# adaLN block on one Trainium2 core: how the first layer norm of the third and fourth chunks is turned from rows into columns

## The chip, the cores and the metric

The kernel runs on one core of a Trainium2 chip. The metric is the device time of one execution in microseconds (us): the median of several runs. The profile is one execution, recorded by the hardware profiler. Engines are named as the profile names them: PE is TensorE's matmul side and PEld its weight load, DVE is VectorE, ACT is ScalarE, POOL is GpSimd, SP is SyncE, which issues every DMA here.

## The reference

```python
x = A_x                                          # 1 x 2048 x 512, fp32
sa, ca, ga, sb, cb, gb = silu(c) @ w_mod         # six vectors of 512
h = layernorm(x) * (1 + ca) + sa
q, k, v = h @ wqkv                               # 32 heads of 16
phi = lambda t: where(t > 0, t + 1, exp(t)) + 1e-6
kv = einsum("bhsd,bhse->bhde", phi(k), v);  z = sum over s of phi(k)
o = (phi(q) @ kv) / (phi(q) . z + 1e-6)
x = x + ga * (o @ wo)
h = layernorm(x) * (1 + cb) + sb
x = x + gb * (((h @ w_gate) * (h @ w_up)) @ w_down)
```

## The kernel before

The 2048 tokens are four chunks of 512 (`NCH`), each of four tiles of 128 tokens (`NJ`); a tile is 128 partitions by 512 features. Tile number i runs from 0 to 15 and is `ch, j = divmod(i, 4)`. Every matrix product is done in three matmuls of high and low parts: an operand f is split into h, its rounded copy (fp32r), and l = f - h, and the product is hh + hl + lh (`product`, L207 to L209). So each operand costs one copy and one subtraction, which ACT, DVE or POOL do.

The order of the work on every engine is written out by hand: the program text is the order, each engine takes its own instructions strictly in that order, and semaphores join the engines. All SBUF tiles come from one pool of 94 buffers (`NB`). PSUM has four banks from `bank()` and four accumulators from `acc_bank()`.

The change lies in the loop over i (L525 to L587), the key stage. An iteration i does, in this order:

- PE: the projection of the keys of tile i + 2 (`proj(i + 2, wk)`, 12 matmuls), in iterations 3, 4, 6 and 7 also that of the queries of one of tiles 0 to 3 (12 matmuls), and `t_tile(i)` (12 matmuls, L373 to L375), which adds x-hat times phi(k) of tile i to the four accumulators.
- ACT and DVE: `k_split_x(i + 1)` and `k_split(i + 1)`, the parts of x-hat and of phi(k) that `t_tile(i + 1)` reads (L194, L195, L364, L365); `k_phi(i + 2)`, which makes phi of the projected keys (two ACT instructions, L337 and L338, and DVE L341); the same for the queries (`q_a`, `q_b`); and `z_add`, the running sum of phi(k) (DVE L358).
- `extra[i]`: work for later stages, such as the splits of `wv` (iterations 4 to 7), the sums for the modulation vectors (`mod_part`, DVE L162 and L164), the loads for them (`mod_load`, on SP's queue) and the splits of `wo`.

`proj` reads a chunk's modulated, transposed rows as pairs (h, l) in `norm[ch].t[k]`, one pair for each of four blocks of 128 features. The first projection that reads chunk 2 is `proj(8, wk)` in iteration 6, and the first that reads chunk 3 is `proj(12, wk)` in iteration 10. Each begins with block k = 0 and takes three matmuls for a block.

How a later chunk's pairs come about, before (chunk 2 in iterations 2 to 5, chunk 3 in 6 to 9):

1. In iteration j = 2 of the chunk two ahead of it, DVE takes the statistics of its tiles 0 and 1, and at j = 3 of tiles 2 and 3 (`stats`, L242 and L243). Then POOL makes the four reciprocal standard deviations at once (`rstd_of`, L262 and L263), DVE the four products with the mean (`nmr_of`, L267), and ACT x-hat of tiles 0 and 1 (`xhat`, L272).
2. At j = 0 of the chunk before it, ACT makes x-hat of tiles 2 and 3.
3. At j = 0 and at j = 1 (`turn_at`, `turn_x`), between the first six and the last six matmuls of `t_tile`, PE transposes two feature blocks of the four tiles, eight matmuls of 128 by 128 (L293), into two PSUM banks; ACT reads each bank once with scale and bias (L305), DVE makes h (L313) and l (L316).

In later stages the kernel already turns other tiles without PE: `stow` and `unstow`, or `move_out` and `move_in`, send a tile to DRAM and read it back in another order of its 32 by 32 blocks; DVE transposes each block in place (L736, L901; the tile `wide` holds a chunk), and `flipped` (L907) lets ACT read one feature block out of `wide` with scale and bias. `xhat_blocks` (L279) writes x-hat with its columns grouped for that.

After the loop the tail of the stage scales the accumulators (L655, L656), splits them (L658 to L660) and multiplies them with `wv` (L667), while PE is covered by `proj(6, wq)` and `proj(7, wq)`.

Of the kernel before, what the change touches and what calls it, by code (L numbers as in the profile page):

```python
# [14 lines left out]
P = 128  # L15
NB = 94
BL = 32
# [7 lines left out]
def tile_adaln_block(  # L25
# [291 lines left out]
                self.t[k] = (h, l)  # L317


    NT = NCH * NJ  # L320
    norm = [Norm(xts[0])]
    wk, wq, wv = [], [], []
# [20 lines left out]
    def k_split_x(i):  # L343
        ch, j = divmod(i, NJ)
        kx[i] = [B("xh", dt=F32R), B("xl", dt=F32R)]
        split(norm[ch].n[j], *kx[i])

    def k_phi(i, ps):
        phi = B("phi")
# [154 lines left out]
    def mod_part(v, *ks):  # L504
        if 0 in ks:
# [11 lines left out]
             12: lambda: (mod_part(4, 2, 3), wo_s.extend(split_raw(x) for x in raw_o[:2]), cols.update({3: col_out(3, mod_col(accs[3], bank()), 0.0)}), mod_load(5)),  # L517
             13: lambda: (mod_part(5, 0, 1, 2), wo_s.extend(split_raw(x) for x in raw_o[2:]), cols.update({4: col_out(4, mod_col(accs[4], bank()), 1.0)})),
             14: lambda: (mod_part(5, 3),)}
    pairs = {}  # L520
    q_at = {3: 0, 4: 1, 6: 2, 7: 3}
    ahead = {2: k_ps[2], 3: k_ps[3]}
    turn_at = {4 * ch + j: (ch + 1, 2 * j, 2 * j + 1) for ch in range(1, NCH - 1) for j in range(2)}
    turn_at.update({1: (1, 0, 1), 2: (1, 2, 3)})
    for i in range(NT):  # L525
        ch, j = divmod(i, NJ)
        done = 0
        if i > 2:
            ahead[i + 2] = proj(i + 2, wk) if i + 2 < NT else proj(i + 6 - NT, wq)
        if i in q_at:  # L530
# [7 lines left out]
        fresh = i > 0 and ch + 1 < NCH and j == 0  # L538
        if i == 2:
            turn_x()  # L540
            wq.extend(split_blocks(r) for r in raw_q)
        if fresh:
            nx.xhat(2)
        if 0 < i < NT - 1:
            k_split_x(i + 1)
        if fresh:
            nx.xhat(3)
        if 0 < i < NT - 1:
            k_split(i + 1)
        if i in turn_at and i != 2:  # L550
            t_tile(i, 0, 1)
            done = 2
            turn_x()
        if i == 2:
            t_tile(i, *range(KD))
            done = KD
            ahead[i + 2] = proj(i + 2, wk)
        if ch + 2 < NCH and j == 2:
            nx2 = Norm(xts[ch + 2])
            nx2.stats(0, 1)  # L560
        if ch + 2 < NCH and j == 3:
            nx = nx2
# [12 lines left out]
        if i + 1 < NT:  # L575
            z_add(i + 1)
        if i == NT - 2:
            pairs["z"] = split_raw(zacc, low=nc.gpsimd)
        if i == NT - 1:
            zps = row_sum(pairs["z"])  # L580
            zb = consts.tile([P, D], F32, name="zb")
            nc.scalar.activation(zb, zps, AF.Identity, bias=eps_z)
            zq = B("z")
            nc.gpsimd.tensor_copy(zq.rearrange("p (q s i) -> p q s i", q=NQ, i=BL), by_block(zb))
        t_tile(i, *range(done, KD))
        if i in extra:
            extra[i]()  # L587
    ga, sb, cb = rows[2], cols[3], cols[4]
# [130 lines left out]
    def move_out(*tiles):  # L719

        for i in tiles:
            moved[i] = tc.dram_tile([P, D], F32, name=f"moved_{i}")
            nc.sync.dma_start(moved[i], phq.pop(i))

    def move_in(*tiles):

        for i in tiles:
            v = moved[i].rearrange("(m i) (q c) -> q i m c", i=BL, c=P)
            moved[i] = B("u")
            for q in range(NQ):  # L730
                nc.sync.dma_start(moved[i][q * BL:(q + 1) * BL].rearrange("i (m c) -> i m c", c=P), v[q])

    def turn_v(i):

# [163 lines left out]

    def flip(ch, *js):
        for j in js:  # L900
            nc.vector.transpose(wide[:, j].rearrange("p (m s i) -> p m s i", m=NQ, i=BL),  # L901
                                blocks.pop((ch, j)).rearrange("p (m s i) -> p m s i", m=NQ, i=BL))

    def flipped(ch, *ks):
        for k in ks:
            f = B("f")
            nc.scalar.activation(f.rearrange("p (x i) -> p x i", i=BL),  # L907
                                 wide.rearrange("p j (m s i) -> p (j m) s i", m=NQ, i=BL)[:, :, k],
                                 AF.Identity, scale=cb[:, k:k + 1], bias=sb[:, k:k + 1])
            blocks[ch, "f", k] = f  # L910

    stowed, blocks = {}, {}

# [403 lines left out]
    first[0].sum("s1", "s3", on=nc.gpsimd)  # L1317
    g(lambda: turn_v(13))
    y_seed(13, y_bank)
    norm2[2].xhat_blocks(2, 3)  # L1320
    turn_h(13)
    turn_l(13)
    move_in(14, 15)
    stow(2, 0, 1, 2, 3)
# [107 lines left out]
```

## Time and profile before

| | us |
|---|---|
| median of 3 runs (554.28 to 555.3) | 554.39 |
| the profiled execution's own time | 554.37 |
| its span, first to last instruction | 552.7 |
| PE busy in the span | 547.0 |
| DVE busy | 373.6 |
| ACT busy | 291.7 |
| POOL busy | 203.4 |

The span is the stretch from the first to the last instruction that the profiler saw, and the 1.67 us beside it are the start and the end of the execution. Busy time is the union of an engine's instructions. A row of the timeline gives the start, the duration, the engine, the line of the kernel, what it writes and reads, and in brackets how long the engine had been idle before it and who ended that. Instructions of one engine overlap by about a tenth of a microsecond at their edges, so the distance from one start to the next is what counts in a queue.

### The profile page before, as it was taken

What the parts mean: (1) busy time and instruction counts of PE and PEld (TensorE: products, weight loads), DVE (VectorE), ACT (ScalarE), POOL (GpSimd) and SP (SyncE); (2) the same over time, 40 slices, a digit from 0 to 9 for tenths busy, and PEclk for the clock granted to TensorE, in tenths of its full rate; (3) what the DMA queues carried; (4) which work ended last, traced back from release to release, by engine and by line L of the source; (5) the groups of instructions that cost most, each with busy time, mean ns of one, the idle gap of its engine ahead of it and who ended that gap; (6) DMA issues with size and microseconds to landing.
All of it is one profiled execution on the core that took longest, in us unless ns stands there. A gap on an engine that the chain in (4) does not pass through costs nothing.

```text
span 552.7 us, 7324 instructions
## 1 busy us (share of the span) xinstructions
PE 547.0 (99%) x2488; PEld 449.2 (81%) x2488; DVE 373.6 (68%) x610; ACT 291.7 (53%) x539; POOL 203.4 (37%) x204
## 2 busy tenths in 40 slices
PE   8999999999999999999999999999999999999997
PEld 7788888888888878878888888877888888888886
DVE  7896968986887886778776576985444444434434
ACT  3695856646476667566684545454443444444110
POOL 2000000102003201057596666766666546446200
PEclk9999999999999999999999999999999999999999
DMA  8900203320503205845545071690434222200004
GB/s 284 387 15 2 76 20 103 108 77 1 157 2 133 96 5 186 267 145 135 160 111 155 0 230 38 216 322 2 133 116 132 59 57 59 58 20 0 1 0 152
DMA packets 58373, 58.28 MB, mean 105 GB/s; under 512 B 7328, under 2 KB 38304, under 8 KB 58336
## 3 DMA queue, kind: packets, MB, share of 16 engines
q1 hardware_dynamic: 58336, 57.83, 33.2%
q8 instruction: 19, 0.31, 0.2%
q14 instruction: 18, 0.15, 0.1%
HBM read 42.60 MB, written 15.20 MB: 105 GB/s over the span
## 4 chain that ended last, share of the span: by engine, by line
PE 99%; DVE 0%; issue 0%
PE bank L1030 33%; PE acc L766 7%; PE acc L1110 6%; PE acc L1111 6%; PE acc L1112 6%; PE bank L207 5%; PE bank L209 5%; PE bank L208 5%; PE acc L375 3%; PE acc L374 3%; PE acc L373 3%; PE bank L849 2%; PE bank L851 2%; PE bank L850 2%; PE acc L146 2%; PE bank L293 2%
## 5 line engine op out<-in xcount | busy, mean ns | idle before, releaser
L1030 PE MATMUL bank<-h,w 128*128 128x512 f32 (+1 forms) x798 | 184.7, 390 | 0.0
L1030 PEld LDWEIGHTS bank<-h,w 128*128 128x128 f32 (+1 forms) x798 | 148.4, 186 | 33.4 <-ACT bank L1035 0.7
L1035 ACT ACTIVATE bank<-bank 128x512 f32<-128x512 f32 (+1 forms) x38 | 22.2, 583 | 139.6 <-PE bank L1030 139.5
L836 DVE TENSOR_TENSOR x<-acc,x 128x512 f32<-128x512 f32 (+1 forms) x73 | 48.8, 682 | 48.4 <-PE acc L1112 47.7
L1016 POOL TENSOR_TENSOR w<-raw,w 128x256 fp32r<-128x256 f32 (+3 forms) x38 | 40.9, 1077 | 91.0 <-ACT w L1009 91.0
L1111 PE MATMUL acc<-w,kh 128*128 128x512 f32 (+2 forms) x154 | 59.6, 387 | 0.0
L1110 PE MATMUL acc<-w,kh 128*128 128x512 f32 (+2 forms) x154 | 59.6, 387 | 0.0
L1112 PE MATMUL acc<-w,kl 128*128 128x512 f32 (+2 forms) x154 | 59.5, 386 | 0.0
L263 POOL TENSOR_TENSOR rstd<-ve,half 128x4 f32<-128x4 f32 (+1 forms) x10 | 11.0, 1103 | 121.8 <-DVE ve L262 69.6
L195 POOL TENSOR_TENSOR w<-raw,w 128x512 fp32r<-128x512 f32 (+1 forms) x25 | 35.1, 1409 | 52.2 <-ACT w L194 47.3
L1016 POOL TENSOR_TENSOR w<-t,w 128x512 fp32r<-128x512 f32 (+1 forms) x38 | 49.2, 1318 | 0.0
L195 DVE TENSOR_TENSOR kl<-u,kh 128x512 fp32r<-128x512 f32 (+1 forms) x38 | 26.4, 736 | 30.6 <-ACT kh L194 30.6
L207 PE MATMUL bank<-w,h 128*128 128x512 f32 x104 | 40.9, 394 | 0.0
L209 PE MATMUL bank<-w,h 128*128 128x512 f32 x104 | 40.6, 391 | 0.0
L208 PE MATMUL bank<-w,h 128*128 128x512 f32 x104 | 40.6, 390 | 0.0
L766 PE MATMUL acc<-w,xh 128*128 128x512 f32 x120 | 37.4, 393 | 0.0
L1089 DVE TENSOR_TENSOR u<-bank,u 128x512 f32<-128x512 f32 (+1 forms) x19 | 13.1, 691 | 31.6 <-PE bank L1030 25.1
L1110 PEld LDWEIGHTS acc<-w,kh 128*128 128x128 f32 (+1 forms) x154 | 28.9, 188 | 6.0
L1112 PEld LDWEIGHTS acc<-w,kl 128*128 128x128 f32 (+1 forms) x154 | 28.9, 188 | 5.9
L1111 PEld LDWEIGHTS acc<-w,kh 128*128 128x128 f32 (+1 forms) x154 | 28.9, 188 | 5.9
L998 POOL TENSOR_TENSOR t<-raw,t 128x256 f32<-128x256 f32 (+1 forms) x34 | 25.9, 761 | 1.4
L766 PEld LDWEIGHTS acc<-w,xh 128*128 128x128 f32 x120 | 22.2, 188 | 4.6
(211 smaller groups left out, 1116.5 us busy)
## 6 DMA issues: line engine op xcount, KB each, us to landing
raw<-in_w_mod_dram SPq DMA_DIRECT2D x24, 256.0 KB, 3.7
raw<-in_B_w_down_dram SPq DMA_DIRECT2D x20, 256.0 KB, 3.2
raw<-in_B_w_gate_dram SPq DMA_DIRECT2D x36, 128.0 KB, 3.4
raw<-in_B_w_up_dram SPq DMA_DIRECT2D x36, 128.0 KB, 3.4
x<-in_A_x_dram SPq DMA_DIRECT2D x16, 256.0 KB, 5.4
out_dram<-x SPq DMA_DIRECT2D x15, 256.0 KB, 2.6
raw<-in_A_wqkv_dram SPq DMA_DIRECT2D x12, 256.0 KB, 5.4
moved<-h SPq DMA_DIRECT2D x12, 256.0 KB, 2.1
```

The source lines that it names most:

```text
L195: (low or nc.vector).tensor_tensor(l, src, f32(h), op=ALU.subtract)
L207: nc.tensor.matmul(ps, ah, bh, start=i == 0, stop=False)
L208: nc.tensor.matmul(ps, ah, bl, start=False, stop=False)
L209: nc.tensor.matmul(ps, al, bh, start=False, stop=i == n - 1)
L766: nc.tensor.matmul(yps[i], x, y, start=False, stop=k == KD - 1 and x is al, skip_group_check=True)
L836: nc.vector.tensor_tensor(xt[:, a:b], dn[j][:, a:b], xt[:, a:b], op=ALU.add)
L998: sub = lambda out, x, y: (on or nc.gpsimd).tensor_tensor(out, x, y, op=ALU.subtract)
L1016: sub = lambda out, x, y: (on or nc.gpsimd).tensor_tensor(out, x, f32(y), op=ALU.subtract)
L1030: mm = lambda x, y, **kw: nc.tensor.matmul(ps, x[:, k], y, skip_group_check=True, **kw)
L1110: nc.tensor.matmul(ps, hh[:, a:b], dh[:n, c:d], start=i == 0, stop=False)
L1111: nc.tensor.matmul(ps, hh[:, a:b], dl[:n, c:d], start=False, stop=False)
L1112: nc.tensor.matmul(ps, hl[:, a:b], dh[:n, c:d], start=False, stop=i == len(hs) - 1)
```

## The change

For chunks 2 and 3 (`LIFTED`), and for them alone, the 16 PE transposes of each chunk go. Their x-hat is written in grouped form by `xhat_blocks`, sent to DRAM (`lift_out`) and read back with its blocks exchanged (`lift_in`, four DMAs a tile), transposed by DVE into `wide` (`lift_turn`), and read by ACT with scale and bias (`lift_row`), after which `lift_parts` makes h (on ACT, or on DVE for the odd blocks of chunk 2) and l (on DVE).

The reciprocal standard deviations and their products are made in halves, for tiles 0 and 1 first. The DVE transposes of tiles 0 and 1 stand at the end of the iteration j = 0, those of tiles 2 and 3, with all four rows and their parts, in the iteration j = 1, behind `k_split` and ahead of `k_phi`. `k_split_x` reads the grouped x-hat through a permuted view. In iteration 6 the query projection `proj(2, wq)` stands ahead of `proj(8, wk)`; in iteration 10 nothing stands ahead of `proj(12, wk)`. The splits of `wo` move from iterations 12 and 13 to 14 and 15. Late in the kernel `turn_h(13)` and `norm2[2].xhat_blocks(2, 3)` change places. The other lines of the diff give existing code new names (`move_out`, `move_in`, `flip` and `flipped` call the new functions).

```diff
+    LIFTED = (2, 3)
+    def lift_out(name, x):
+        to = tc.dram_tile([P, D], F32, name=name)
+        nc.sync.dma_start(to, x)
+        return to
+    def lift_in(of):
+        v = of.rearrange("(m i) (q c) -> q i m c", i=BL, c=P)
+        u = B("u")
+        for q in range(NQ):
+            nc.sync.dma_start(u[q * BL:(q + 1) * BL].rearrange("i (m c) -> i m c", c=P), v[q])
+        return u
+    def lift_turn(j, u):
+        nc.vector.transpose(wide[:, j].rearrange("p (m s i) -> p m s i", m=NQ, i=BL),
+                            u.rearrange("p (m s i) -> p m s i", m=NQ, i=BL))
+    def lift_row(k, scale, shift):
+        f = B("f")
+        nc.scalar.activation(f.rearrange("p (x i) -> p x i", i=BL),
+                             wide.rearrange("p j (m s i) -> p (j m) s i", m=NQ, i=BL)[:, :, k],
+                             AF.Identity, scale=scale[:, k:k + 1], bias=shift[:, k:k + 1])
+        return f
+    def lift_parts(k, f, cast=True):
+        h, l = B("h", dt=F32R), B("h", dt=F32R)
+        if k % 2 and cast:
+            nc.vector.tensor_copy(h, f)
+        else:
+            nc.scalar.activation(h, f, AF.Copy)
+        nc.vector.tensor_tensor(l, f, f32(h), op=ALU.subtract)
+        return h, l
...
-        split(norm[ch].n[j], *kx[i])
+        if ch not in LIFTED:
+            split(norm[ch].n[j], *kx[i])
+            return
+        x = by_row(norm[ch].n[j])
+        h, l = (t.rearrange("p (s q i) -> p s q i", q=NQ, i=BL) for t in kx[i])
+        nc.scalar.activation(h, x, AF.Copy)
+        nc.vector.tensor_tensor(l, x, f32(h), op=ALU.subtract)
...
-             12: lambda: (mod_part(4, 2, 3), wo_s.extend(split_raw(x) for x in raw_o[:2]),
-             13: lambda: (mod_part(5, 0, 1, 2), wo_s.extend(split_raw(x) for x in raw_o[2:]),
-             14: lambda: (mod_part(5, 3),)}
+             14: lambda: (mod_part(5, 3), wo_s.extend(split_raw(x) for x in raw_o[:2])),
+             15: lambda: wo_s.extend(split_raw(x) for x in raw_o[2:])}
-    turn_at = {4 * ch + j: (ch + 1, 2 * j, 2 * j + 1) for ch in range(1, NCH - 1) for j in range(2)}
-    turn_at.update({1: (1, 0, 1), 2: (1, 2, 3)})
+    turn_at = {1: (1, 0, 1), 2: (1, 2, 3)}
     for i in range(NT):
+        up = ch + 1 if 0 < ch < NCH - 1 else None
+        if i == 6:
+            qps = proj(q_at[i], wq)
         if i > 2:
             ahead[i + 2] = proj(i + 2, wk) if i + 2 < NT else proj(i + 6 - NT, wq)
-        if i in q_at:
+        if i in q_at and i != 6:
             qps = proj(q_at[i], wq)
...
-        if fresh:
-            nx.xhat(2)
+        if ch + 2 < NCH and j == 3:
+            nx = nx2
+            nx.nmr_of(0, 2)
+            nx.xhat_blocks(0, 1)
+            lifts = [lift_out(f"first_{ch}_{n}", nx.n[n]) for n in range(2)]
         if 0 < i < NT - 1:
             k_split_x(i + 1)
-        if fresh:
-            nx.xhat(3)
-        if 0 < i < NT - 1:
             k_split(i + 1)
+        if up and j == 1:
+            lift_turn(2, lifts[2])
+            lift_turn(3, lifts[3])
+            for k in range(KD):
+                nx.t[k] = lift_parts(k, lift_row(k, ca, sa), cast=up == 2)
+            norm[up:] = [nx]
...
         if ch + 2 < NCH and j == 2:
             nx2 = Norm(xts[ch + 2])
             nx2.stats(0, 1)
+            nx2.rstd_of(0, 2)
         if ch + 2 < NCH and j == 3:
-            nx = nx2
             nx.stats(2, 3)
-            nx.rstd_of()
-            nx.nmr_of()
-            nx.xhat(0, 1)
+            nx.rstd_of(2, 4)
...
+        if ch + 2 < NCH and j == 3:
+            nx.nmr_of(2, 4)
+            nx.xhat_blocks(2, 3)
+            lifts[0], lifts[1] = lift_in(lifts[0]), lift_in(lifts[1])
+            lifts += [lift_out(f"first_{ch}_{n}", nx.n[n]) for n in (2, 3)]
+            lifts[2], lifts[3] = lift_in(lifts[2]), lift_in(lifts[3])
...
+        if up and j == 0:
+            lift_turn(0, lifts[0])
+            lift_turn(1, lifts[1])
         if i in extra:
             extra[i]()
```

More of the change, by code (lines that the diff above doesn't have):

```diff
@@ L516, in tile_adaln_block @@
              11: lambda: (mod_part(3, 3), mod_part(4, 0, 1), rows.update({2: mod_row(2, pairs[2])}), raw_o.extend(load(wo_v[k], "raw") for k in range(2, KD))),
-             12: lambda: (mod_part(4, 2, 3), wo_s.extend(split_raw(x) for x in raw_o[:2]), cols.update({3: col_out(3, mod_col(accs[3], bank()), 0.0)}), mod_load(5)),
-             13: lambda: (mod_part(5, 0, 1, 2), wo_s.extend(split_raw(x) for x in raw_o[2:]), cols.update({4: col_out(4, mod_col(accs[4], bank()), 1.0)})),
-             14: lambda: (mod_part(5, 3),)}
+             12: lambda: (mod_part(4, 2, 3), cols.update({3: col_out(3, mod_col(accs[3], bank()), 0.0)}), mod_load(5)),
+             13: lambda: (mod_part(5, 0, 1, 2), cols.update({4: col_out(4, mod_col(accs[4], bank()), 1.0)})),
+             14: lambda: (mod_part(5, 3), wo_s.extend(split_raw(x) for x in raw_o[:2])),
+             15: lambda: wo_s.extend(split_raw(x) for x in raw_o[2:])}
     pairs = {}
@@ L536, in turn_x @@
             norm[to:] = [nx]
-        fresh = i > 0 and ch + 1 < NCH and j == 0
         if i == 2:
@@ L721, in move_out @@
         for i in tiles:
-            moved[i] = tc.dram_tile([P, D], F32, name=f"moved_{i}")
-            nc.sync.dma_start(moved[i], phq.pop(i))
+            moved[i] = lift_out(f"moved_{i}", phq.pop(i))
     def move_in(*tiles):
         for i in tiles:
[L728 to L731, printed above, removed]
+            moved[i] = lift_in(moved[i])
     def turn_v(i):
@@ L900, in flip @@
         for j in js:
-            nc.vector.transpose(wide[:, j].rearrange("p (m s i) -> p m s i", m=NQ, i=BL),
-                                blocks.pop((ch, j)).rearrange("p (m s i) -> p m s i", m=NQ, i=BL))
+            lift_turn(j, blocks.pop((ch, j)))
     def flipped(ch, *ks):
         for k in ks:
[L906 to L910, printed above, removed]
+            blocks[ch, "f", k] = lift_row(k, cb, sb)
     stowed, blocks = {}, {}
@@ L1319, in tile_adaln_block @@
     y_seed(13, y_bank)
+    turn_h(13)
     norm2[2].xhat_blocks(2, 3)
-    turn_h(13)
     turn_l(13)
```

## The prediction

> **What bounds the kernel now.** I read the busy shares and the chain of the page, then who makes PE wait, then the timeline of the key stage by engine.
>
> ```profile
> PE 547.0 (99%) x2488; PEld 449.2 (81%) x2488; DVE 373.6 (68%) x610; ACT 291.7 (53%) x539; POOL 203.4 (37%) x204
> PEclk9999999999999999999999999999999999999999
> PE 99%; DVE 0%; issue 0%
> ```
>
> PE alone makes up the chain, at its full clock. What makes PE wait is a list of one row, the very first matmul:
>
> ```profile
> PE acc L146 <- DVE w L141: 2.0, 1, 2.0
> ```
>
> So PE is never late, and two things alone can move the end: PE's own work, and a new wait of PE. The timeline of PE:
>
> ```profile
> 55.79 1.03 PE L293 MATMUL bank<-ident,n 128*128 128x128 f32 x8
> 56.58 0.48 PE L373 MATMUL acc<-kh,xh 128*128 128x512 f32 x1
> 56.90 0.39 PE L374 MATMUL acc<-kh,xl 128*128 128x512 f32 x1
> ...
> 64.39 0.39 PE L207 MATMUL bank<-w,h 128*128 128x512 f32 x1
> ...
> 93.65 0.39 PE L207 MATMUL bank<-w,h 128*128 128x512 f32 x1
> ...
> 96.37 0.39 PE L373 MATMUL acc<-kh,xh 128*128 128x512 f32 x1
> ```
>
> One 128x512 matmul takes 0.227 us from start to start, a projection of twelve 2.72 (93.65 to 96.37). Iteration 6 begins at 64.39; proj(12), the first reader of chunk 3, begins at 93.65 and is over at 96.37.
>
> How late are the other engines already? In the next rows DVE's last l of chunk 2 ends at 65.80, and PE wants it for the last matmul of proj(8) at 64.39 + 11 x 0.227 = 66.89; chunk 3's ends at 95.06 and is wanted at 93.65 + 2.50 = 96.15. Both margins are 1.1 us.
>
> ```profile
> 65.11 0.69 DVE L316 TENSOR_TENSOR h<-f,h 128x512 fp32r<-128x512 f32 x1
> 65.72 0.68 DVE L341 SCALAR_TENSOR_TENSOR phi<-bank,phi 128x512 f32<-128x512 f32 x1
> ...
> 68.73 0.69 DVE L242 BATCH_NORM_STATS2 st<-x 128x6 f32<-128x512 f32 x1
> 69.45 0.18 DVE L243 BATCH_NORM_AGGREGATE mv<-st 128x2 f32<-128x6 f32 x1
> 69.55 0.66 DVE L242 BATCH_NORM_STATS2 st<-x 128x6 f32<-128x512 f32 x1
> ...
> 94.37 0.69 DVE L316 TENSOR_TENSOR h<-f,h 128x512 fp32r<-128x512 f32 x1
> ```
>
> **What goes.** Four groups of eight transposes. A group costs PE 56.90 - 55.79 - 0.23 = 0.88 us, its slow successor included: 3.5 us in all. It is gained only where PE then meets no wait.
>
> **What comes: prices.** All of it is done elsewhere in this kernel.
>
> ```profile
> 64.12 0.60 ACT L337 ACTIVATE phi<-bank 128x512 f32<-128x512 f32 x1
> 64.75 0.63 ACT L338 ACTIVATE phi<-phi 128x512 f32<-128x512 f32 x1
> 65.28 0.62 ACT L194 ACTIVATE w<-raw 128x512 fp32r<-128x512 f32 x1
> 65.81 0.61 ACT L194 ACTIVATE xh<-n 128x512 fp32r<-128x512 f32 x1
> 66.44 0.72 ACT L364 ACTIVATE kh<-phi,eps_phi 128x512 fp32r<-128x512 f32 x1
> ```
>
> ```profile
> 315.63 0.81 ACT L907 ACTIVATE f<-wide,col,col 128x512 f32<-128x512 f32 x1
> ```
>
> ```profile
> 77.73 1.52 ACT L272 ACTIVATE n<-x,nmr,rstd 128x512 f32<-128x512 f32 x2 [4.71 <-DVE nmr L267]
> ```
>
> ```profile
> 301.49 1.30 DVE L901 STREAM_TRANSPOSE wide<-u 128x512 f32<-128x512 f32 x2
> 302.71 0.65 DVE L1175 TENSOR_TENSOR raw<-raw,row 128x512 f32<-128x512 f32 x1
> ```
>
> ```profile
> 44.36 0.18 DVE L243 BATCH_NORM_AGGREGATE mv<-st 128x2 f32<-128x6 f32 x1
> ```
>
> ```profile
> 48.91 1.01 POOL L263 TENSOR_TENSOR rstd<-ve,half 128x4 f32<-128x4 f32 x1 [19.53 <-DVE ve L262]
> ```
>
> ```profile
> 49.95 0.16 DVE L267 SCALAR_TENSOR_TENSOR nmr<-mv,rstd 128x4 f32<-128x4 f32 x1 [1.21 <-POOL rstd L263]
> ```
>
> Steps in a queue, start to start: DVE 0.60 for a 128x512 operation, 0.61 for a transpose (two in 1.22), 0.81 for the statistics of a tile (68.73 to 69.55); ACT 0.71 for x-hat (two in 1.52, one of them 0.81) and for a row out of wide, 0.52 for a copy, 0.63 for kh, 1.16 for the two parts of phi; 0.83 where the next one reads a row just made (0.80 and the 0.03 between 64.12 + 0.60 and 64.75). ve is priced as the product beside it, 0.16. Halves cost one POOL power and one product more a chunk; for two columns I take the 1.01 of four.
>
> **The sum, as one chain.** The new order chains ACT and DVE together; PE appears in it nowhere. Times are on the clock of before; the first half of chunk 2's statistics ends at 44.5, as now (the row at 44.36).
>
> - ve, power, product: ACT starts x-hat 0 and 1 at 46.1; then xh, kh, to 48.6. DVE takes kl at 48.7, two tiles of statistics and ve, to 51.2; the power, to 52.3; ACT makes x-hat 2 and 3 from 52.6, xh, kh and two phis, to 57.6.
> - DVE from 57.6: phi and z (1.2), two transposes (1.2), the wv part, xl and kl (1.8), two transposes: 63.1. ACT only now begins its rows: h of block 0 at 64.6, of block 2 at 66.7, the last row at 66.6 to 67.4; DVE's last copy and l take 1.2 more, to 68.6.
> - PE reaches proj(8) at 64.39 - 1.76 + 2.72 (the query projection ahead) = 65.35 and would end it at 68.1; the last l holds it to 69.0. **Loss 1.0** for chunk 2, against 1.76 gained.
> - ACT's phi(7) ends at 68.6. DVE: phi, z, wv, xl, kl (3.0), two statistics and ve, to 73.4; phi, phi of q, z, wv (2.4); only then chunk 3's product, 75.8. ACT has been idle since 73.1; from 76.0 x-hat 0 and 1, xh, kh, to 78.6, two phis to 81.0. DVE: kl at 78.7, two statistics, ve 81.2, POOL 82.3.
> - ACT from 82.5: x-hat 2 and 3, wv, xh, kh, phi(10), to 86.9. DVE: phi, z (1.2), two transposes (1.2), L162 and L164 (1.2), xl, kl (1.2), two transposes: 93.0.
> - ACT: a row and its copy, 0.83 + 0.52 = 1.35 a block: h at 94.5, 95.8, 97.2, 98.5; the last l at 99.3. A weight load ahead of its matmul takes 0.2, so proj(12) ends near 99.8.
>
> Before, it ended at 96.37. **Loss 3.4 us**, whatever PE saved: it would be ready at 93.65 - 3.5 + 1.0 = 91.1, waits 3.6 us for h of block 0, and then in each block, which takes PE three matmuls, 0.68, and ACT 1.35. Behind it the next keys come from what PE does next, and nothing of the loss returns. The query projection put ahead delays the bank of proj(8) by 2.72, to 69.2, while ACT reaches it at 70.2: nothing.
>
> **DMAs.** Each lift writes a tile, then SP issues four reads, in SP's order both tiles of a half behind each other.
>
> ```profile
> moved<-h SPq DMA_DIRECT2D x12, 256.0 KB, 2.1
> u<-moved SPq DMA_DIRECT2D x48, 64.0 KB, 2.0
> ```
>
> ```profile
> 173.70 1.82 SPq L731 DMA_DIRECT2D u<-moved  x4
> ```
>
> x-hat 2 and 3 of chunk 3 are done at 84.0; tile 2 is written by 85.5, eight reads are issued by 89.1 (two times 1.82), the last lands at 91: DVE comes for tile 3 at 92.3. Hidden by 1.3 us, chunk 2's by about as much. mod_load(3) stands behind these reads on SP and goes out at 89 to 91; its reader on DVE stands behind phi of proj(12), 9 us later, four times what a lift needs to land. Uncovered, a late read would cost its lateness one for one.
>
> **The rest.** k_split_x reads a permuted view; on ACT the row out of wide does that at x-hat's price, on DVE split_blocks does at the usual 0.69:
>
> ```profile
> L226 DVE TENSOR_TENSOR w<-raw,w x4: 684/684/684, 39.2 to 41.0; 128x512 fp32r<-128x512 f32 x4
> ```
>
> The wo splits in iteration 15 fall ahead of the tail:
>
> ```profile
> 131.73 2.49 DVE L195 TENSOR_TENSOR w<-n,w 128x512 fp32r<-128x512 f32 x4
> ```
>
> ```profile
> 127.89 2.41 ACT L655 ACTIVATE n<-acc,col 128x512 f32<-128x512 f32 x4
> ```
>
> ```profile
> 135.66 0.27 PE L208 MATMUL bank<-w,w 128*128 128x128 f32 x1
> ```
>
> ACT's two copies now stand at 127.89, ahead of L655, and DVE's two subtractions behind the first of them: the tail slips by 1.2 (two subtractions) to 1.8 (with the wait for a copy). Its last l goes from 134.2 to between 135.4 and 136.0, and PE wants it at 135.66, for the weights 0.2 earlier: **loss 0 to 0.6, I take 0.3**, the middle. The pair in iteration 14 falls into idle time. The swap of turn_h(13) moves one ACT copy past two x-hats: 0, at most 0.6; no wait of PE stands there. Four more buffers a chunk, out of 94, make SP's reads wait for work of an iteration or more before: 0, and a late one would count as a late read.
>
> Sum: 554.37 + 3.4 + 0.3 = **558.1 us**. The profiled execution's 554.37 stands 0.02 from the median.
>
> **Rivals.**
> 1. *The waits stay covered.* Faster: 554.37 - 3.5 = 550.9. For it, ACT was idle 4.71 us for the product of chunk 3's four tiles, which halves shorten (the row at 77.73). It decides at chunk 3's last l: ready by 92.4 gives all, 3.4 us before my 99.3 gives a draw. Against it: the transposes, which PE gave early, now stand behind xl and kl. Chance 0.07.
> 2. *The queues catch up by iteration 8*, and phi(10) is set by PE: iteration 8 begins 72 matmuls after 64.39, at 80.7; the bank is full at 80.7 - 1.76 + 1.0 + 2.72 + 0.2 = 82.9, DVE starts phi at 84.2 instead of 86.9, and proj(12) ends at 97.1: 554.37 + 0.7 + 0.3 = 555.4. It asks that the chain from 44.5 to 86.9 take 2.7 us (6%) less than its steps add up to, all of them taken from rows. Chance 0.14.
> 3. *The clock.* If 3.6 us of idleness lowers PE's clock, the next twelve matmuls at half speed cost 2.7 more: 560.8. No row of before shows PE idle so long or a lower clock. The Trainium skill, "TensorE: Matmul & The Clock Gate", "Part 1: The HAM clock gate", halves the clock after one idle window of about 3.4 us; by that this is near the edge. Chance 0.07.
> 4. *Late reads* add up to 1.5: 559.6. Chance 0.07.
>
> **How the numbers follow.** The forecast, 557 to 559.5, has 0.65. The range, 555.3 to 560.8, holds it, rivals 3 and 4 and half of rival 2. 0.2% is 1.1 us, about what a measurement tells from none: faster is rival 1, 0.07; the same is half of rival 2, 0.07; slower 0.86.
>
> **What would show it.** PE's waits list h of L351 and l of L352, over 5 us together, most at proj(12); ACT idle before the first row of each chunk, ended by DVE wide; DVE's last transpose of chunk 3 near 93 and the last l near 99.3, DMA ending none of DVE's idleness. I am wrong if PE meets these matmuls without a wait, or if DVE and ACT stand more than 3 us earlier at chunk 3's rows.

## The result and the profile after

| | median us | lowest to highest | runs |
|---|---|---|---|
| before | 554.47 | 554.12 to 555.76 | 6 |
| after | 558.36 | 558.0 to 560.53 | 6 |

The ratio is 1.0071, with a 95% interval of 1.0052 to 1.009: the change costs 3.9 us. The interval lies above 1, so the change makes the kernel slower, by 0.7%. The execution of after that was profiled took 558.0, its span is 556.3. In some executions, the profiled ones of runs 1, 2, 4 and 12 below among them, PE's clock is also halved for 3.41 us near 16 us, all that follows starts 0.8 to 1.7 us later, and medians of a few runs move by some tenths with it. The row of busy time and the chain of the page, to be set beside those of before:

```profile
PE 546.8 (98%) x2456; PEld 446.3 (80%) x2456; DVE 377.9 (68%) x616; ACT 295.3 (53%) x545; POOL 203.8 (37%) x206
PE 95%; DVE 2%; ACT 1%; issue 1%; DMA 0%; DVEq 0%; ACTq 0%
```

The 32 transposes have left PE (2488 to 2456 instructions), DVE has got 4.3 us and ACT 3.6, and the chain is no longer PE alone. What makes PE wait, in a list that had one row before (line, what for, sum, times, longest):

```profile
PE bank L207 <- ACT h L351: 3.5, 1, 3.5
PE acc L146 <- DVE w L141: 2.0, 1, 2.0
```

The timeline of PE shows where. These rows are the first matmul of proj(8) and the first one behind it; then the last matmul of iteration 9's own products, the first two rows of proj(12) that begin a block, and the first one behind it:

```profile
65.21 0.39 PE L207 MATMUL bank<-w,h 128*128 128x512 f32 x1
...
68.70 0.39 PE L414 MATMUL acc<-kh,xh 128*128 128x512 f32 x1
...
90.39 0.39 PE L416 MATMUL acc<-kl,xh 128*128 128x512 f32 x1
94.27 0.50 PE L207 MATMUL bank<-w,h 128*128 128x512 f32 x1 [3.50 <-ACT h L351]
...
95.64 0.79 PE L207 MATMUL bank<-w,h 128*128 128x512 f32 x1
...
99.47 0.39 PE L414 MATMUL acc<-kh,xh 128*128 128x512 f32 x1
```

At 0.227 a matmul, proj(8) would be over at 67.93 and is over at 68.70: 0.77 lost, in gaps too short for the list of waits. proj(12) could begin at 90.62, begins at 94.27, and takes 5.20 instead of 2.72, as ACT hands it a block every 1.37. It was over at 96.37 before and is over at 99.47 now. This execution runs 0.2 earlier up to there (iteration 3 begins at 48.69, not 48.89), so the loss is 3.3.

What PE waits for is on ACT, in a queue that had nothing to do for 4.66 us before it:

```profile
75.73 1.52 ACT L279 ACTIVATE n<-x,nmr,rstd 128x512 f32<-128x512 f32 x2 [2.99 <-DVE nmr L267]
...
92.75 0.81 ACT L341 ACTIVATE f<-wide,col,col 128x512 f32<-128x512 f32 x1 [4.66 <-DVE wide L336]
93.59 0.63 ACT L351 ACTIVATE h<-f 128x512 fp32r<-128x512 f32 x1
94.13 0.80 ACT L341 ACTIVATE f<-wide,col,col 128x512 f32<-128x512 f32 x1
```

And what ACT waits for is on DVE, behind the splits of x and of the keys:

```profile
67.62 0.69 DVE L352 TENSOR_TENSOR h<-f,h 128x512 fp32r<-128x512 f32 x1
...
75.53 0.15 DVE L267 SCALAR_TENSOR_TENSOR nmr<-mv,rstd 128x2 f32<-128x2 f32 x1
...
90.15 0.68 DVE L387 TENSOR_TENSOR xl<-n,xh 128x512 fp32r<-128x512 f32 x1
90.75 0.68 DVE L406 SCALAR_TENSOR_TENSOR kl<-phi,kh 128x512 fp32r<-128x512 f32 x1
91.36 1.30 DVE L336 STREAM_TRANSPOSE wide<-u 128x512 f32<-128x512 f32 x2
94.25 0.69 DVE L352 TENSOR_TENSOR h<-f,h 128x512 fp32r<-128x512 f32 x1 [1.60 <-ACT h L351]
...
98.36 0.69 DVE L352 TENSOR_TENSOR h<-f,h 128x512 fp32r<-128x512 f32 x1 [0.68 <-ACT h L351]
```

Read upwards from PE this is one line of handovers. Neither engine is full in it, as the table of windows has it (stretch, its length, then busy time and instructions of PE, PEld, DVE, ACT and POOL, PE's granted clock, the DMAs' share and rate): DVE works for 12.77 of 16.60 us, ACT for 10.15.

```profile
76.00:92.60 16.60, 14.77 (x65) 11.83 (x63) 12.77 (x24) 10.15 (x17) 0.70 (x1) 1.00 0.51 164
```

One thing is new that no row of before has. In the same view of after, PE's clock is 0.50 for 3.41 us of proj(12):

```profile
92.24:95.65 3.41, 1.24 (x4) 0.49 (x4) 1.13 (x3) 2.84 (x5) 0.00 (x0) 1.00 0.97 335
95.65:99.06 3.41, 3.41 (x8) 2.06 (x8) 2.05 (x3) 3.31 (x6) 0.00 (x0) 0.50 0.39 138
```

So three causes stand against each other: **the chain** (the queues of ACT and DVE reach chunk 3's rows too late; PE's clock and the DMAs only look on), **the clock** (the idle time halves PE's clock, and that is the loss), **late reads** (the way through memory), and beside them that the added work costs its length wherever it stands.

### The profile page after: what moved, and what is told of

Same layout as the page of the kernel before. It is cut to its first block, busy times and chain, and to the rows that moved or that the text cites. A ratio compares the mean times of both kernels' runs of the same rounds, so it can differ in the third digit from the quotient of the medians.

```text
span 556.3 us, 7368 instructions
## 1 busy us (share of the span) xinstructions
PE 546.8 (98%) x2456; PEld 446.3 (80%) x2456; DVE 377.9 (68%) x616; ACT 295.3 (53%) x545; POOL 203.8 (37%) x206
## 4 chain that ended last, share of the span: by engine, by line
PE 95%; DVE 2%; ACT 1%; issue 1%; DMA 0%; DVEq 0%; ACTq 0%
PE bank L1077 33%; PE acc L818 7%; PE acc L1157 6%; PE acc L1159 6%; PE acc L1158 6%; PE bank L207 4%; PE bank L209 4%; PE bank L208 4%; PE acc L416 2%; PE acc L415 2%; PE acc L414 2%; PE bank L903 2%; PE bank L901 2%; PE bank L902 2%; PE acc L146 2%; PE acc L928 1%
## 5 line engine op out<-in xcount | busy, mean ns | idle before, releaser
L263 POOL TENSOR_TENSOR rstd<-ve,half 128x2 f32<-128x2 f32 (+1 forms) x12 | 11.7, 978 | 125.3 <-DVE ve L262 73.1
L207 PE MATMUL bank<-w,h 128*128 128x512 f32 x104 | 42.2, 406 | 3.6 <-ACT h L351 3.5
L209 PE MATMUL bank<-w,h 128*128 128x512 f32 x104 | 41.5, 399 | 0.0
L208 PE MATMUL bank<-w,h 128*128 128x512 f32 x104 | 41.1, 396 | 0.0
L207 PEld LDWEIGHTS bank<-w,h 128*128 128x128 f32 x104 | 19.8, 191 | 9.2 <-ACT h L351 5.1
```

The costliest lines, as they stand in the source:

```text
L207: nc.tensor.matmul(ps, ah, bh, start=i == 0, stop=False)
L208: nc.tensor.matmul(ps, ah, bl, start=False, stop=False)
L209: nc.tensor.matmul(ps, al, bh, start=False, stop=i == n - 1)
```

## The experiments

Beside the times, the table gives three moments of the profiled execution, each counted from its own start of iteration 3 (the first matmul of proj(5)): the first matmul of proj(12), the first one behind proj(12), and the row sum behind the tail's products (L183). Each ratio is to a median of before that was measured along with the run, 554.39 to 554.66.

| kernel | median us | ratio to before (95%) | proj(12) begins | is over | tail |
|---|---|---|---|---|---|
| before | 554.39 | | 44.76 | 47.48 | 91.01 |
| after | 558.36 | 1.0071 (1.0052 to 1.009) | 45.58 | 50.78 | 94.71 |
| 1 chunk 2 alone | 556.51 | 1.0032 (1.0017 to 1.0048) | 45.79 | 48.51 | 92.42 |
| 2 chunk 3 alone | 557.43 | 1.005 (1.0037 to 1.0063) | 43.98 | 49.15 | 93.08 |
| 3 chunk 3 alone, earlier | 552.99 | 0.9971 (0.9963 to 0.9979) | 42.94 | 45.66 | 89.19 |
| 4 no moves | 558.55 | 1.0074 (1.0059 to 1.0088) | 45.51 | 51.06 | 95.18 |
| 5 two more turns | 559.64 | 1.0093 (1.008 to 1.0106) | 47.04 | 52.59 | 96.71 |
| 6 PE kept busy | 558.47 | 1.0069 (1.0057 to 1.0081) | 45.58 | 50.74 | 94.68 |
| 7 odd copies on DVE | 558.63 | 1.0071 (1.0058 to 1.0084) | 45.58 | 50.54 | 94.46 |
| 8 splits back | 557.8 | 1.0057 (1.0045 to 1.0069) | 45.57 | 50.82 | 94.38 |
| 9 q behind | 559.14 | 1.0085 (1.0072 to 1.0098) | 46.19 | 51.36 | 95.29 |
| 10 copies and busy | 557.99 | 1.0059 (1.0047 to 1.0071) | 45.59 | 49.89 | 93.82 |
| 11 both, chunk 3 earlier | 553.31 | 0.9984 (0.9974 to 0.9994) | 43.27 | 46.03 | 89.56 |
| 12 turns first | 558.71 | 1.0069 (1.0057 to 1.0081) | 44.33 | 49.57 | 94.00 |

**1 and 2: one chunk each.** The edit of run 1, beside the code that lets the other chunk go by PE as before; run 2 has `(3,)`, and no query projection ahead in iteration 6:

```diff
-    LIFTED = (2, 3)
+    LIFTED = (2,)
```

> Only chunk 2 is turned by VectorE; chunk 3 is turned by PE in iterations 8 and 9 as in the kernel before, and its four x-hat tiles wait for one product as there. Theory (one chain of handovers between ACT and DVE sets the end of each chunk's rows): PE saves two groups, 1.76 us, waits about 0.8 at proj(8), as after, and is then handed chunk 3's x-hat late, because the turning of chunk 2 keeps the queues of ACT and DVE late through iterations 6 and 7: a new wait of PE of about 2 us for x-hat ahead of its transposes near 85 to 87. With 0.3 for the tail: about 556.0. Rival (the two chunks add up, each with its own wait): 554.5 - 1.76 + 0.8 + 0.3 = 553.8, and no wait of PE at its transposes. Rival (work added to ACT and DVE costs its length wherever it stands): half of the 3.9 us, 556.4, spread over the loop.

> Only chunk 3 is turned by VectorE; chunk 2 is turned by PE in iterations 4 and 5 as in the kernel before, and the query projection of iteration 6 stands behind proj(8) as there. Theory (one chain): the queues come to chunk 3 about 2 us earlier than after, since chunk 2 didn't hold them, but the order of steps in iterations 7 to 9 is the same: h of block 0 about 1.3 us late for proj(12), the blocks then at ACT's pace of 1.35; proj(12) ends near 98, time about 556.3. Rival (each chunk has its own wait): the whole of the waits at proj(12), 3.1 us net of what was saved, stays: 557.5 or more. Rival (DMA late): DVE's idle time ahead of its transposes ends with a DMA.

PE's waits with chunk 2 alone, and the rows of ACT's timeline behind them:

```profile
PE bank L293 <- ACT n L272: 1.6, 2, 0.9
```

```profile
81.04 1.52 ACT L272 ACTIVATE n<-x,nmr,rstd 128x512 f32<-128x512 f32 x2 [5.47 <-DVE nmr L267]
...
85.28 0.80 ACT L272 ACTIVATE n<-x,nmr,rstd 128x512 f32<-128x512 f32 x1
```

As the chain has it: chunk 2, which loses 0.8 us at its own proj(8), makes chunk 3's x-hat late, and PE stands ahead of its transposes. The tail moment is 1.41 later than before (the chain's 1.5). The median, 556.51, lies by the 556.4 of the second rival; the trace decides against it, since the loss is not spread over the loop but stands in two places, proj(8) and these transposes. With chunk 3 alone, PE's list of waits has:

```profile
PE bank L207 <- ACT h L351: 0.9, 1, 0.9
```

proj(12) waits for block 0 and then goes at ACT's pace, 5.17 long at full clock (43.98 to 49.15). It is over 1.67 later than before, the tail is 2.07 later, against 1.8 by the chain and 3.0 by its rival. The ratio's interval, 2.1 to 3.5 us, lies nearer to the rival; the trace, which leaves the late start out, decides for the chain. At the end of proj(12) the two alone lose 1.03 and 1.67, together 2.70 of the 3.30 of after: each loses by itself, so no single one of them can be undone to mend it.

**3: the same work, earlier.** Chunk 3's steps move from iterations 6 to 9 to iterations 5 to 8, its rows to the head of iteration 9; odd copies go to DVE and the output projection's splits back to 12 and 13.

```diff
+        if i == 5:
+            ny = Norm(xts[3])
+            ny.stats(0, 1)
+            ny.rstd_of(0, 2)
...
+        if i == 9:
+            for k in range(KD):
+                ny.t[k] = lift_parts(k, lift_row(k, ca, sa))
+            norm[3:] = [ny]
         if 0 < i < NT - 1:
             k_split_x(i + 1)
```

> As the run with chunk 3 alone, with the same operations for chunk 3, but every step of it one iteration earlier: statistics in iterations 5 and 6, x-hat and the moves in 6, transposes in 7 and 8, the rows of wide at the head of iteration 9, odd copies on DVE; the output projection's splits back in iterations 12 and 13. Theory (lateness in the queues, not the work): h and l are ready before proj(12) wants them, PE meets no wait and keeps the two groups it saves: 554.5 - 1.8 = 552.7. Rival (the work itself, added to ACT and DVE, costs): no faster than the run with chunk 3 alone, about 556. Rival (the clock or the DMAs): between, 554 to 555, with a lower granted clock or idle time ended by DMAs.

PE's list of waits is the one row of before again. From the timelines of ACT, DVE and PE in run 3: ACT's first row out of wide, DVE's last l, PE's first matmul of proj(12):

```profile
87.27 0.82 ACT L341 ACTIVATE f<-wide,col,col 128x512 f32<-128x512 f32 x1 [1.93 <-DVE wide L336]
```

```profile
92.31 0.69 DVE L352 TENSOR_TENSOR h<-f,h 128x512 fp32r<-128x512 f32 x1
```

```profile
92.04 0.39 PE L207 MATMUL bank<-w,h 128*128 128x512 f32 x1
```

The last l ends at 93.00 and is wanted at 92.04 + 2.50 = 94.54. The same operations for chunk 3, with 1.5 us in hand, cost nothing, and PE keeps 1.82 at proj(12) and at the tail. So the work as such isn't the loss; its place is. (Run 3 also has the odd copies on DVE and the splits back, which runs 10 and 8 price at 0.9 and 0.4; its proj(12) is over 3.5 sooner than that of run 2.) At 552.99 (ratio 0.9971, 0.9963 to 0.9979) this kernel beats before and after.

**4: no moves.** The kernel leaves out the way through memory of the eight tiles of chunks 2 and 3: `lift_out` and `lift_in` (with `True`) hand on the tile itself.

```diff
     def lift_out(name, x):
+        if name.startswith("first"):
+            return x
...
-            lifts[0], lifts[1] = lift_in(lifts[0]), lift_in(lifts[1])
+            lifts[0], lifts[1] = lift_in(lifts[0], True), lift_in(lifts[1], True)
...
```

> The changed kernel without its moves through memory: the sixteen tiles' writes and reads for the regrouping are left out, and VectorE turns x-hat where it stands, so the keys and queries of chunks 2 and 3 get elements out of order; every other operation is as in the changed kernel. Theory (one chain of ACT and DVE; a move takes less than the time that DVE takes to come to it): no change, 558.4 within 0.4. Rival (late reads): each half's reads hold up DVE by up to 1.5 us, so 557 or less, and proj(12) ends over 1 us earlier.

DVE's timeline in run 4, the second pair of transposes:

```profile
92.36 1.30 DVE L340 STREAM_TRANSPOSE wide<-n 128x512 f32<-128x512 f32 x2
```

Without the moves the second pair of transposes starts 42.65 us after iteration 3 does; with them, 42.67 (91.36 - 48.69). proj(12) begins 0.07 sooner. So late reads are no cause of the loss of after. proj(12) is over 0.28 later: in this run the half clock lasted 6.83 us.

**5: two more turns.**

```diff
         if up and j == 1:
+            if up == 3:
+                for _ in range(2):
+                    lift_turn(2, lifts[2])
             lift_turn(2, lifts[2])
```

> The changed kernel with two more transposes on VectorE: tile 2 of chunk 3 is turned three times instead of once in iteration 9, into the same place. Theory (DVE's transposes, ACT's rows and PE's proj(12) are one chain without slack): their 2 x 0.61 arrive at PE one for one; h of block 0 and the end of proj(12) 1.2 us later than after, 559.6. Rival (ACT's rows or a late read set the end, DVE has slack there): less than 0.4 later, 558.4 to 558.8. Rival (clock): PE idle for 4.7 us in a row instead of 3.5 lowers the clock for longer, and the next matmuls cost 0.7 or more on top: 560.3 or more.

The same place on DVE's timeline in run 5:

```profile
91.24 2.79 DVE L336 STREAM_TRANSPOSE wide<-u 128x512 f32<-128x512 f32 x4
```

Four transposes take 2.79, two took 1.30: 1.49 more, not the 1.22 that I had worked out. proj(12) begins 1.46 later: one for one, DVE has no slack there. Its end is 1.81 later: here too the clock was halved for 6.83 us, longer than in after, as the rival on the clock has it. That is not free: from the first matmul of proj(12) to the tail, runs 4 and 5 both take 49.67, after 49.13. The median, 559.64, is nearer to the theory's 559.6 than to the rival's 560.3.

**6, 7 and 10: the clock.** Run 6 gives PE fourteen matmuls in place of the wait, run 7 moves two copies from ACT to DVE, run 10 does both.

```diff
+            if i == 10:
+                padded = bank()
+                for _ in range(14):
+                    nc.tensor.matmul(padded, wk[0][0][:, :P], wk[0][0], start=True, stop=True)
-            ahead[i + 2] = proj(i + 2, wk) if i + 2 < NT else proj(i + 6 - NT, wq)
+            ahead[i + 2] = proj(i + 2, wk, (lambda: padded) if i == 10 else bank) if i + 2 < NT else proj(i + 6 - NT, wq)
...
-                nx.t[k] = lift_parts(k, lift_row(k, ca, sa), cast=up == 2)
+                nx.t[k] = lift_parts(k, lift_row(k, ca, sa), cast=True)
```

> The changed kernel with fourteen 128x512 matmuls ahead of proj(12), into the bank that proj(12) then starts afresh, so that PE is busy for 3.2 of the 3.5 us in which it waits for h of block 0. Theory (ACT's and DVE's lateness sets the end; the half clock of 3.41 us falls where PE waits for ACT in each block, and is mostly hidden): the granted clock stays at 1.0 there, h comes at the same time, proj(12) ends within 0.2 of 99.5; the median falls by 0 to 0.4, to 558.0 to 558.4, and the runs at a clock of 0.991 to 0.994 are gone. Rival (the clock): the half clock is a real part of the loss, and without it the time falls by 1 us or more, 557.4 or less.

> The changed kernel with the copies of blocks 1 and 3 of chunk 3 made by VectorE, as those of chunk 2 are. Theory (within proj(12), ACT's row and copy of each block, 1.35 us, set the pace): ACT is relieved of two copies of 0.52, block 3's h comes about 0.9 us sooner: proj(12) ends near 98.6, time 557.5. Rival (DVE sets the pace, or the first block's wait alone counts): no change, 558.4, or later, since DVE then makes two copies and four subtractions behind its transposes.

> The changed kernel with both: the odd copies of chunk 3 on VectorE, and fourteen matmuls ahead of proj(12) into its bank. With the odd copies alone the half clock became the pace: proj(12) took 4.96 us from 94.11 to 99.07, and twelve matmuls at 0.43 are 5.16. Theory (ACT's row and copy set the pace as long as PE has its full clock; the lower clock hid what the copies gave): at the full clock proj(12) ends 0.7 to 0.9 earlier than with the matmuls alone, 557.6, with the clock at 1.0 there. Rival (DVE's copies and subtractions set the pace, the clock nothing): proj(12) again takes about 5 us, 558.3.

PE's list of waits in run 6:

```profile
PE bank L207 <- ACT h L351: 0.3, 1, 0.3
```

The 3.5 us of waiting for h have become 0.3, the clock is 1.00 throughout, and every moment of the table is that of after within 0.04: with the full clock nothing is won. The median, 558.47, is no lower than that of after (558.0 to 558.4 was expected). In after, ACT hands over a block in 1.37 us and PE at half clock needs 3 x 0.43 = 1.29 for it. So the clock is not what makes after slower.

In run 7 block 0 comes when it did, and proj(12) takes 4.96, only 0.24 less than in after where I had expected 0.9. The half clock in the windows of run 7:

```profile
95.54:98.95 3.41, 3.41 (x9) 2.43 (x9) 3.15 (x6) 3.14 (x6) 0.00 (x0) 0.50 0.37 114
```

In the 3.41 us PE now has nine matmuls at work instead of eight, most of them 0.43 apart, where in after the second matmul of each block came 0.51 to 0.59 behind the first: the blocks now come faster than PE takes them at half clock, and this takes most of the win. With the full clock, run 10, proj(12) takes 4.30 instead of 5.16 (run 6): the 0.86 that the copies are worth is there, and the time is 557.99, 0.4 under after in the median and 0.7 in the lowest run (557.34 to 558.0). Run 7's median is no better than after's: three of its runs, at a mean clock of 0.991, took 559.2 to 559.6, and three, at 0.997, 557.6 to 558.1.

**8: the splits back in iterations 12 and 13.**

```diff
-             12: lambda: (mod_part(4, 2, 3), cols.update(...
+             12: lambda: (mod_part(4, 2, 3), wo_s.extend(split_raw(x) for x in raw_o[:2]), cols.update(...
...
-             15: lambda: wo_s.extend(split_raw(x) for x in raw_o[2:])}
```

> The changed kernel with the splits of the output projection's weights back in iterations 12 and 13, where the kernel before has them. Theory: DVE's and ACT's chain ahead of the tail is two subtractions shorter; the stretch from the start of the query projection of iteration 15 to the products of the tail shrinks by 0.2 to 0.4 us, with no wait of PE in it: 558.1. Rival (hidden): no change of that stretch, 558.4. Rival (the splits in iterations 12 and 13 now collide with what the late iteration 9 left over): PE waits there, 558.4 or more.

From the end of proj(12) to the tail: 43.93 in after (94.71 - 50.78), 43.56 here, 43.53 before. The splits' place cost 0.4, and no wait of PE replaced it.

**9: the query projection behind proj(8).**

```diff
-    q_at = {3: 0, 4: 1, 6: 2, 7: 3}
+    q_at, q_ahead = {3: 0, 4: 1, 6: 2, 7: 3}, ()
...
-        if i == 6:
+        if i in q_ahead:
             qps = proj(q_at[i], wq)
...
-        if i in q_at and i != 6:
+        if i in q_at and i not in q_ahead:
             qps = proj(q_at[i], wq)
```

> The changed kernel with the query projection of iteration 6 behind proj(8) again, nothing else. Theory (the chain of ACT and DVE sets when chunk 3's rows are ready, PE appears in it nowhere): PE waits about 2.3 us for h of block 0 of chunk 2 at proj(8), makes the query projection behind it, comes to proj(12) later by nearly as much, and waits there only about 1.3 us instead of 3.5; proj(12) ends where it ended: 558.4 within 0.4. Rival (each wait of PE is a loss of its own): the 2.3 us come on top, 560.5 or more.

PE's list of waits in run 9:

```profile
PE bank L207 <- ACT h L351: 2.8, 3, 1.8
```

The longest, 1.8, is the one at proj(8); proj(12) begins only 1.27 after the matmul ahead of it instead of 3.88. So most of the new wait was taken out of the old one, against the rival. But proj(12) comes 0.6 later than in after, and this the chain as I had it excludes. ACT's timeline in run 9 shows where the 0.6 arises:

```profile
76.09 1.52 ACT L279 ACTIVATE n<-x,nmr,rstd 128x512 f32<-128x512 f32 x2 [1.78 <-DVE nmr L267]
...
80.80 0.60 ACT L372 ACTIVATE h<-bank 128x512 f32<-128x512 f32 x1 [0.90 <-PE bank L209]
...
86.28 0.60 ACT L372 ACTIVATE phi<-bank 128x512 f32<-128x512 f32 x1 [0.22 <-PE bank L209]
```

The first row, x-hat of chunk 3's tiles 0 and 1, is not late: it starts 27.00 after iteration 3 does, in after 27.04. The delay comes behind it, in two places where ACT waits for a bank of PE. The phi of iteration 7's query waits 0.90, and through DVE's part of it the product for tiles 2 and 3 and their x-hat come 0.27 later. Then phi(10) waits 0.22 and starts 37.19 after iteration 3 instead of 36.61; from there on everything is 0.6 later. So PE does appear in the chain as soon as it is late enough.

How late PE was is partly the clock's doing. In run 9 the clock is halved from 65.59 to 69.00, and proj(8) is over 0.43 later than in after (20.44 against 20.01 behind the start of iteration 3), though its last l came as early. With PE 0.43 sooner, by these rows, the first delay would be nothing and the second about 0.15: this is an estimate, and no run has this order at full clock.

**11: both chunks, chunk 3 earlier.** Run 3, with chunk 2 by DVE too, and query projections in iterations 3, 6, 7 and 10, those of 6 and 10 ahead. Unlike the text on record, the edit puts chunk 2's second pair of transposes ahead of both splits, not between them. In part:

```diff
-    q_at = {3: 0, 4: 1, 6: 2, 7: 3}
+    q_at, q_ahead = {3: 0, 6: 1, 7: 2, 10: 3}, (6, 10)
...
+        if i == 5:
+            lift_turn(2, lifts[2])
+            lift_turn(3, lifts[3])
+        if i == 9:
+            lift_rows(*(0, 1, 2, 3))
         if 0 < i < NT - 1:
             k_split_x(i + 1)
             k_split(i + 1)
...
```

> Both chunks turned by VectorE: chunk 3 as in the faster run, one iteration earlier with its rows at the head of iteration 9; chunk 2 at its place, its second pair of transposes between the splits of x and of the keys; query projections ahead in iterations 6 and 10, the others in 3 and 7; the output projection's splits in 12 and 13. Theory (a chunk's turning pays only where ACT and DVE come in time, which chunk 2's cannot since its statistics begin no sooner): PE still waits about 1.1 us for h of block 0 at proj(8) and then goes at ACT's pace to a last l near 67.4, about 2 us lost for 1.76 saved; chunk 3 keeps its saving: 553.4, no better than chunk 3 alone. Rival (earlier order frees both): 551.3.

Measured 553.31, tail 0.37 behind run 3: chunk 2 saves 1.76, so it loses 2.1. PE's wait for block 0 at proj(8) is 0.4 instead of the 1.1 expected; the rest is lost within proj(8), which takes 4.31 (62.86 to 67.17) instead of 2.72. The reads, hidden in after, are no longer so, now that DVE comes sooner (DVE's timeline in run 11):

```profile
60.58 0.71 DVE L336 STREAM_TRANSPOSE wide<-u 128x512 f32<-128x512 f32 x1 [0.63 <-DMA u<-first]
```

This turn of tile 3 starts 1.32 after that of tile 2 (59.26) instead of 0.61. What chunk 2 would lose without the late read, run 11 doesn't show.

**12: the turns first.** In iteration 9 alone, the second pair of transposes and the rows move ahead of k_split_x and k_split.

```diff
+        if up == 3 and j == 1:
+            lift_turn(2, lifts[2])
+            lift_turn(3, lifts[3])
...
         if 0 < i < NT - 1:
             k_split_x(i + 1)
             k_split(i + 1)
-        if up and j == 1:
+        if up == 2 and j == 1:
...
```

> The changed kernel with chunk 3's second pair of transposes and its rows ahead of the splits of x and keys in iteration 9, nothing else. Theory (the transposes stand behind xl and kl on DVE, two steps of 0.61): DVE comes to the second pair 1.2 us sooner, h of block 0 is 1.1 us sooner; the splits of tile 10 come later and hold PE up behind proj(12) by about 0.5: 557.8. Rival (late reads: DVE would now wait for tile 3's read): h of block 0 no sooner, DVE's idle time ahead of the transposes ended by a DMA, 558.4 or more.

DVE's timeline in run 12, where the transposes now follow the product of L164:

```profile
90.97 0.75 DVE L164 SCALAR_TENSOR_TENSOR f<-raw,sc,f 128x512 f32<-128x512 f32 x1
91.64 1.29 DVE L336 STREAM_TRANSPOSE wide<-u 128x512 f32<-128x512 f32 x2
```

proj(12) begins 1.25 sooner and is over 1.21 sooner, two steps of DVE; no DMA ends idle time of DVE there. Behind it the products of tile 10 take 3.19 instead of 2.75, waiting for the splits put back. Net 0.71 at the tail, as expected. The median, 558.71, doesn't show it; the two runs with the least of the half clock (mean clock 0.996 and 0.997) took 557.65 and 557.69, where the runs of after at 0.997 took 558.0 to 558.16.

## Why the prediction was right

Forecast 558.1, measured 558.36, by the mechanism that it named. The forecast adds 3.4 + 0.3 = 3.7 to before; in the traces the tail comes 3.70 later (94.71 - 91.01). Step by step, on the clock of before (after's rows plus 0.2):

| step | predicted | measured |
|---|---|---|
| last l of chunk 2 | 68.6 | 68.5 |
| proj(8) is over | 69.0 | 68.9 |
| chunk 3's first product | 75.8 | 75.7 |
| chunk 3's transposes are over | 93.0 | 92.9 |
| h of block 0 | 94.5 | 94.4 |
| last l of chunk 3 | 99.3 | 99.25 |
| proj(12) is over | 99.8 | 99.7 |

- **What goes**, 0.88 us of PE a group: run 3 removes two groups with no wait and gains 1.82, against 1.76.
- **Loss of chunk 2**, 1.0 (by its own steps, 69.0 less 68.1, 0.9): measured 0.77. Run 1 adds what I had only as part of one chain: this chunk also delays chunk 3's x-hat, whoever turns it.
- **Loss of chunk 3**, 3.4: 3.3. The prices, all of them rows of other places of before, held: a row and its copy 1.35 a block, measured 1.37; steps of 0.60 and 0.61 on DVE.
- **"PE appears in it nowhere"** was too strong. It holds in after, where PE is ahead of the queues; in run 9 late banks hold up ACT, and proj(12) comes 0.6 later; by the estimate above most of it goes back to the half clock at proj(8).
- **The query projection ahead, "nothing"**: right for the bank of proj(8). With the projection behind proj(8) instead, proj(12) comes 0.6 later, the half clock of that run included.
- **DMAs hidden by 1.3**: run 4 moves proj(12) by 0.07 when they are gone. Run 12, where DVE comes to the second pair 1.19 sooner (41.48 after the start of iteration 3), still meets no late read, so they were hidden by at least that. The reads were issued when I had said, up to 89.1 (SP's timeline in after):

```profile
85.15 3.98 SPq L332 DMA_DIRECT2D u<-first  x8
```

- **The signs**: ACT's idle time before the first rows and DVE's and ACT's moments came as named, but not PE's list of waits. It has 3.5 us for h of L351 and no row for l of L352, where over 5 was forecast; the rest is lost in gaps too short for the list, 0.77 in proj(8) and 5.20 - 2.72 = 2.48 in proj(12).
- **The tail**, 0 to 0.6, taken as 0.3: 0.4 by run 8. The swap of turn_h(13): from the tail's row sum to PE's last matmul 408.89 before (548.79 - 139.90), 408.88 after (552.28 - 143.40): nothing.
- **Rival 1** (waits covered) and **rival 2** (the queues catch up by iteration 8) fell together: DVE's phi(10) stands at 86.57 (86.8 on the clock of before), where the forecast had 86.9 and rival 2 84.2; rival 4 fell with run 4.
- **Rival 3** (the clock) came true as an event and not as a price. I had put twelve matmuls at half speed at 2.7 us on top; but ACT hands over a block in 1.37 us, so PE would have been idle for most of the time that the half clock takes, and run 6 finds 0.03 (tail 94.71 against 94.68). Where the half clock lasts 6.83 us, as in runs 4 and 5, it costs about 0.5. The Trainium skill, "TensorE: Matmul & The Clock Gate", "Part 1: The HAM clock gate", has the clock halved after an idle window of about 3.4 us in windows that run freely. The traces agree with the free windows: the half clock begins 5.3 us after the last matmul ahead of proj(12) does in after and run 7, but 4.4 after it in run 5 and 2.8 in run 12, and it lasts 3.41 or 6.83. They differ on "idle": the 3.41 us before it had PE busy for 1.24 in after (the row above) and for 1.61 in run 9 (table of windows):

```profile
62.18:65.59 3.41, 1.61 (x7) 0.72 (x5) 1.85 (x4) 2.31 (x4) 0.00 (x0) 1.00 0.76 247
```

Three things stay open: why the 0.1 to 2 us between the runs of one kernel come as they do (the half clock near 16 us is part of it); what a query projection behind proj(8) costs at full clock; and whether chunk 2 can be turned by DVE without loss in some other order; run 11 is one try, with a late read in it.

## What to carry to other kernels

Moving work off the engine that bounds a kernel gains only what the other engines' queues can deliver by the moment the bounding engine wants it: write down that moment and the margin (here 1.1 us), then add up the new chain with every handover. If the sum is late, the same operations an iteration earlier may pay in full, as run 3 does with 1.5 us in hand. And a shorter wait may be hidden by the next limit: the copies were worth 0.86, but only once PE's clock was kept up.

## What the runs showed of the hardware

- PE's clock changes on a grid of 3.413 us that runs through the whole execution: in runs 4 and 12 the two stretches of half clock begin 78.5 us apart (15.79 and 94.30, 16.18 and 94.68), which is 23 times 3.413. The program lies differently on the grid in each execution.
- In the key stage the half clock came behind stretches of this grid in which PE's rows fill 0 to 47% (0.00 of 3.41 us in run 5, 1.24 in after, 1.61 in run 9). It did not come behind one of 52% in run 1, where the clock, the third figure from the end, stays at 1.00:

```profile
84.56:87.97 3.41, 1.77 (x12) 1.21 (x11) 2.51 (x5) 3.41 (x7) 0.00 (x0) 1.00 0.19 48
87.97:91.38 3.41, 3.41 (x17) 2.81 (x16) 3.34 (x7) 2.92 (x5) 0.00 (x0) 1.00 0.10 37
```

- The rows don't show all that counts: in run 1 the half clock near 16 us comes behind 3.41 us (12.88 to 16.29) that PE's rows fill for 3.38, with 24 instructions, 16 of which are matmuls of 128x1 and 4 transposes.
- What 3.41 us of half clock cost depends on what it falls on. At proj(12), where ACT hands over a block every 1.37 us, it cost 0.03 (after against run 6). In run 7, where the blocks come faster than the 1.29 that PE needs at half clock, it is the pace (4.96 against 4.30 in run 10). At proj(8) in run 9 it comes with an end 0.43 later. A half clock of 6.83 us cost about 0.5 (runs 4 and 5).
- In the second 3.41 us of run 4, PE stayed at half clock though it had been busy for 2.49 of the first (table of windows):

```profile
94.30:97.71 3.41, 2.49 (x6) 1.58 (x6) 1.39 (x2) 3.31 (x6) 0.00 (x0) 0.50 0.21 57
97.71:101.12 3.41, 3.41 (x9) 2.24 (x8) 2.05 (x4) 3.16 (x6) 0.00 (x0) 0.50 0.09 34
```

- Two 128x512 transposes of different tiles on DVE start 0.61 apart; each further turn of the same tile into the same place added (2.79 - 1.30) / 2 = 0.75 (run 5).
